# A fused retention and rational feed-forward kernel: in steps 8 to 21, u moves into attention's PSUM banks and the steps get an order of their own

## The chip, the cores and the metric

The kernel runs on one core of one Trainium2 chip. The metric is the device time of one execution in microseconds. Five engines work side by side, each through its own list of instructions in order, and wait for each other by semaphores: TensorE (PE, with its weight loads as PEld) multiplies, VectorE (DVE), ScalarE (ACT) and GpSimd (POOL) work element by element, SyncE (SP) issues the DMAs.

## The reference

Attention without softmax but with a decay, then a feed-forward layer whose activation is a quotient of two polynomials:

```python
scores = scale * np.matmul(q, k.transpose(0, 1, 3, 2))      # 8 x 8 heads, 576 positions of 64
ret = scores * Dmat                                          # gamma ** (i - j) for i >= j, else 0
x = np.matmul(ret, v)                                        # regrouped to 4608 x 512
h = x @ w_in                                                 # 512 -> 2048
P = a[0] + a[1] * h + a[2] * h**2 + a[3] * h**3
Q = 1.0 + np.abs(b[0]) * np.abs(h) + np.abs(b[1]) * h**2
out = (P / (Q + 1e-06)) @ w_out                              # 2048 -> 512
```

## The kernel before

The 4608 rows are 9 blocks of 512 rows. Attention makes x in 36 units of 128 rows, four to a block. The feed-forward layer works block by block (b) and, within a block, through 16 slices of 128 columns of the hidden layer (f). One pair (b, f) is a **step**. The order of the steps is: block 0, f 0 to 7 (steps 0 to 7); block 1, f 0 to 15 (steps 8 to 23); block 0, f 8 to 15 (steps 24 to 31); then blocks 2 to 8. Weights arrive as pairs of float32 words of float64 numbers and have to be put together and split into a high and a low part on the chip; this goes on until step 23, one piece of weight a step.

Operands of the products are kept as high and low parts, so each product is done three times: `gemm1` has 12 matmuls into the PSUM tile h, `gemm2` 12 into acc. PSUM has eight banks: two for h (tile pool `ps_h`, two buffers), four for acc (`ps_acc`), two for attention (`ps_at`, one tile "at" of 2 x 512). No unit of attention is worked on between step 7 and step 22 (list `SCORES`: 5, then 23), so the tile "at" lies unused there.

What one step computes, with the names that the profile shows:

- `ffn_p`: ScalarE writes p<-h (Identity with scale a3 and bias a2) and u<-h (Abs); VectorE p<-p,h (p times h).
- `ffn_p2`: VectorE p<-p,ab_sb,h, after which h's bank is free.
- `ffn_v`: ScalarE v<-u,absb (b1 u + b0), then VectorE v<-v,u (v times u). So v is Q - 1.
- `ffn_r`, for the step before: ScalarE u<-v,lnb (Ln) and u<-u,lnb (Exp): u becomes about 1/Q.
- `ffn_q`, for the step before: VectorE p<-p,ab_sb,u (p becomes P times that), v<-v,u (Q times that), p<-v,p (one Newton step). Below they are q1, q2 and q3.
- `ffn_hi`, `ffn_lo`, for the step before that: ScalarE g<-p rounds p to the high part; the low part g<-p,g is done by GpSimd for the steps up to 23, by VectorE later.
- `gemm2`, three or four steps behind `gemm1` (`lag`).

A piece of weight is prepared by a generator, `split_weight`: `start` is ScalarE's c<-bits; `split0` VectorE's TENSOR_SCALAR c<-c; `split1` VectorE's first c<-bits,c (low word) and `split2` its second (the sign; both have one form); `split3` ScalarE's w<-c and GpSimd's w<-c,w.

The order on each engine is the order in which the code records the instructions: `InOrder` keeps it (line 63, which is why all rows of the profile carry L63). Within a step it is a list of names that `run` goes through: `FIRST` up to step 23, `DENSE` up to step 31, then `REST`, and `END` after the last step. u and v lie in the pool `el` (two buffers in SBUF), p in `el3` (three), g in `gp` (three).

Of the kernel before, what the change touches and what calls it, by code (L numbers as in the profile page):

```python
# [12 lines left out]
F32 = mybir.dt.float32  # L13
# [8 lines left out]
P = 128  # L22
# [7 lines left out]
NF = DFF // P  # L30
# [2 lines left out]
BEFORE = "split1 start scale_q scale_v scores decay outputs split2 add fade keep_hi keep_lo split3 split0".split()  # L33
FIRST = (
    "split1 gemm1 outputs ffn_p split2 ffn_hi keep_hi ffn_lo gemm2 ffn_r scale_q split3 add fade keep_lo start ffn_p2"
    " scale_v scores decay split0 ffn_q ffn_v"
).split()
DENSE = (
    "gemm1 outputs keep_hi split1 add fade keep_lo ffn_p split2 split0 ffn_v scale_q ffn_hi ffn_r ffn_lo scale_v gemm2"
    " ffn_p2 scores decay split3 ffn_q"  # L40
).split()
REST = (
    "gemm1 ffn_p outputs keep_hi add fade keep_lo ffn_hi ffn_p2 ffn_lo scores decay scale_q scale_v ffn_v gemm2 ffn_r ffn_q"
).split()
END = "ffn_r ffn_hi gemm2 ffn_lo ffn_q".split()

STARTS_BEFORE = [0, 1, 1, 2, 2]
STARTS = [1, 1, 2, 1, 2] + [1] * 19
# [1 line left out]
SCORES = [1, 3, 5, 23, 25, 27, 29, *range(2 * NF, (NB - 1) * NF, 4)]  # L50
# [16 lines left out]
def retention_ffn(ctx: ExitStack, tc: tile.TileContext, qkv, w_in, w_out, ab, masks, gq, gv, out):  # L67
# [23 lines left out]
    ps_at = ctx.enter_context(tc.tile_pool(name="ps_at", bufs=1, space=PSUM))  # L91
# [208 lines left out]
    els = {}  # L300
    gs = {}
    accs = {}
    part = []
    spare = {}

# [11 lines left out]
    def ffn_p(b, f):  # L317

        h = hs[b, f]
        u, v, p = els[b, f] = [  # L320
            (el3 if t == "p" else el).tile([P, 512], F32, tag=t, name=f"{t}{b}_{f}") for t in "uvp"
        ]
        act.activation(p, h, AF.Identity, bias=a2, scale=a3)
        act.activation(u, h, AF.Abs)
        dve.tensor_tensor(p, p, h, ALU.mult)
# [2 lines left out]
        p = els[b, f][2]  # L328
        dve.scalar_tensor_tensor(p, p, a1, hs.pop((b, f)), ALU.add, ALU.mult)

    def ffn_v(b, f):

        u, v, p = els[b, f]
        act.activation(v, u, AF.Identity, bias=b0, scale=b1)
        dve.tensor_tensor(v, v, u, ALU.mult)

    def ffn_r(b, f):
# [5 lines left out]
    def ffn_q(b, f):  # L343

        u, v, p = els[b, f]
        dve.scalar_tensor_tensor(p, p, a0, u, ALU.add, ALU.mult)
        dve.scalar_tensor_tensor(v, v, QC, u, ALU.add, ALU.mult)
        dve.scalar_tensor_tensor(p, v, 2.0, p, ALU.subtract, ALU.mult)

    def place(b, f):  # L350
# [54 lines left out]
    half = NF // 2  # L405
    first = half + NF
    runs = [(0, 0, half), (1, 0, NF), (0, half, NF)] + [(b, 0, NF) for b in range(2, NB)]
    steps = [(b, f, f == r0, f == r1 - 1) for b, r0, r1 in runs for f in range(r0, r1)]
    at = {s[:2]: i for i, s in enumerate(steps)}

    def lag(i):

        return 4 if NF // 2 <= i < first - 2 or i >= len(steps) - 8 else 3
# [6 lines left out]
    def load_weights(n):  # L420
        for k in [k for _, k in zip(range(n), loads)]:
            load_weight(k)
# [12 lines left out]
    def run(names, todo):  # L435
        todo |= {f"split{j}": (split_step, j) for j in range(4)}
        for name in names:
            if name in todo:
                todo[name][0](*todo[name][1:])
# [43 lines left out]
    for i in range(len(steps) + lag(len(steps))):  # L483
        this, prev, prev2 = (steps[j][:2] if 0 <= j < len(steps) else None for j in (i, i - 1, i - 2))
        todo = {"gemm2": (products, i), "start": (split_start, STARTS[i] if i < first else 0)}

        out_n = None
        if due and this and i >= due[0][1]:
            out_n = due.pop()[0]
            todo |= {f.__name__: (f, out_n) for f in (keep_hi, add, keep_lo, fade)}  # L490
            todo["outputs"] = (put_out, out_n)
        if i in SCORES:
            todo |= {f.__name__: (f, nxt) for f in (scores, decay)}
            due.append((nxt, i + (1 if i < 2 * NF else 2)))
            nxt += 1
        if i + 1 in SCORES:
            todo |= {f.__name__: (f, nxt) for f in (scale_q, scale_v)}
        if this:
            todo |= {f.__name__: (f, *this) for f in (gemm1, ffn_p, ffn_p2, ffn_v)}
        if prev:  # L500
            todo |= {f.__name__: (f, *prev) for f in (ffn_r, ffn_q)}
        if prev2:
            todo |= {"ffn_hi": (ffn_hi, *prev2), "ffn_lo": (ffn_lo, *prev2, i - 2 < first)}
        run(END if not this else FIRST if i < first else DENSE if i < 2 * NF else REST, todo)
        load_weights(2)


# [48 lines left out]
```

## Time and profile before

| | |
|---|---|
| Median of 3 runs | 981.95 us (980.52 to 983.37) |
| The profiled execution | 983.9 us, its span 982.1 us |
| Mean granted clock of TensorE | 0.980 |
| Busy over the whole span | PE 925.9, DVE 841.0, ACT 712.9, POOL 168.8 us |

A line of the timeline reads: start and length in us, engine, line, operation, output<-inputs by the program's names (without buffer numbers), shape, how many in a row, and in brackets how long the engine sat idle before it and what ended that. A line of groups reads: the same names, count, busy time in us, mean ns of one, idle time before them. A line of stages reads: the stretch, its length, for each engine the busy time and the number of instructions, TensorE's granted clock, the DMA share and GB/s. A line of waits reads: who waited for whom, us in total, how often, the longest.

### The profile page before, as it was taken

What the parts mean: (1) busy time and instruction counts of PE and PEld (TensorE: products, weight loads), DVE (VectorE), ACT (ScalarE), POOL (GpSimd) and SP (SyncE); (2) the same over time, 40 slices, a digit from 0 to 9 for tenths busy, and PEclk for the clock granted to TensorE, in tenths of its full rate; (3) what the DMA queues carried; (4) which work ended last, traced back from release to release, by engine and by line L of the source; (5) the groups of instructions that cost most, each with busy time, mean ns of one, the idle gap of its engine ahead of it and who ended that gap; (6) DMA issues with size and microseconds to landing.
All of it is one profiled execution on the core that took longest, in us unless ns stands there. A gap on an engine that the chain in (4) does not pass through costs nothing.

```text
span 982.1 us, 16128 instructions
## 1 busy us (share of the span) xinstructions
PE 925.9 (94%) x6234; PEld 749.2 (76%) x6234; DVE 841.0 (86%) x1261; ACT 712.9 (73%) x1274; POOL 168.8 (17%) x200
## 2 busy tenths in 40 slices
PE   6669887889999999999999999999999999999997
PEld 6547765667788888888888888888888888888886
DVE  3999988998788988888888888888888888888895
ACT  5477677776766777877787777777777777777775
POOL 4545434344011111101111111101111111100000
PEclk9788999998999999999999999999999999999999
DMA  9945000002212111220121112110211121001001
GB/s 343 407 168 213 3 0 1 1 1 86 86 44 86 44 45 43 87 65 22 44 87 43 44 44 86 44 58 29 87 44 43 44 86 44 2 1 43 0 1 44
DMA packets 20557, 65.44 MB, mean 67 GB/s; under 512 B 2304, under 2 KB 2432, under 8 KB 20480
## 3 DMA queue, kind: packets, MB, share of 16 engines
q1 hardware_dynamic: 20480, 64.41, 18.4%
q8 instruction: 49, 0.80, 0.3%
q14 instruction: 28, 0.23, 0.1%
HBM read 54.96 MB, written 9.44 MB: 66 GB/s over the span
## 4 chain that ended last, share of the span: by engine, by line
PE 77%; DVE 12%; ACT 4%; issue 3%; DMA 2%; POOL 1%; SPq 0%; POOLq 0%; ACTq 0%
PE acc L63 35%; PE h L63 33%; PE ps L63 9%; DVE c L63 6%; DVE p L63 4%; DVE v L63 1%; ACT c L63 1%; DMA kv<-in_qkv 1%; ACT kv L63 1%; POOL w L63 1%; DMA mask_sb<-in_masks 1%; ACT u L63 0%; ACT w L63 0%; ACT o L63 0%; DVE s L63 0%
## 5 line engine op out<-in xcount | busy, mean ns | idle before, releaser
L63 PE MATMUL acc<-w,g 128*128 128x512 f32 x1632 | 404.5, 397 | 5.2 <-ACT o L63 4.0
L63 PE MATMUL h<-xhi,w 128*128 128x512 f32 x1152 | 381.5, 392 | 18.1 <-DVE p L63 16.0
L63 PEld LDWEIGHTS acc<-w,g 128*128 128x128 f32 x1632 | 304.7, 190 | 75.9 <-ACT o L63 4.9
L63 PEld LDWEIGHTS h<-xhi,w 128*128 128x128 f32 x1152 | 217.2, 189 | 69.1 <-DVE p L63 21.0
L63 PE MATMUL h<-xlo,w 128*128 128x512 f32 x576 | 225.4, 391 | 0.2 <-DVE xlo L63 0.2
L63 ACT ACTIVATE p<-h,ab_sb 128x512 f32<-128x512 f32 x144 | 111.4, 773 | 105.9 <-PE h L63 105.8
L63 ACT ACTIVATE u<-h 128x512 f32<-128x512 f32 x144 | 85.9, 596 | 76.6 <-DVE v L63 75.0
L63 DVE SCALAR_TENSOR_TENSOR p<-p,ab_sb,u 128x512 f32<-128x512 f32 x144 | 107.8, 749 | 25.4 <-ACT u L63 22.1
L63 PEld LDWEIGHTS h<-xlo,w 128*128 128x128 f32 x576 | 108.7, 189 | 22.5 <-DVE xlo L63 0.5
L63 DVE TENSOR_TENSOR v<-v,u 128x512 f32<-128x512 f32 x144 | 99.7, 692 | 27.9 <-ACT v L63 27.7
L63 DVE TENSOR_TENSOR p<-p,h 128x512 f32<-128x512 f32 x144 | 98.9, 687 | 27.9 <-ACT u L63 27.4
L63 ACT ACTIVATE v<-u,absb 128x512 f32<-128x512 f32 x144 | 116.0, 805 | 0.3
L63 DVE SCALAR_TENSOR_TENSOR p<-p,ab_sb,h 128x512 f32<-128x512 f32 x144 | 107.1, 744 | 3.1
L63 ACT ACTIVATE u<-u,lnb 128x512 f32<-128x512 f32 x144 | 104.3, 724 | 4.7
L63 DVE SCALAR_TENSOR_TENSOR p<-v,p 128x512 f32<-128x512 f32 x144 | 99.6, 692 | 5.0
L63 ACT ACTIVATE u<-v,lnb 128x512 f32<-128x512 f32 x144 | 102.8, 714 | 0.2 <-DVE v L63 0.2
L63 DVE SCALAR_TENSOR_TENSOR v<-v,u 128x512 f32<-128x512 f32 x144 | 99.2, 689 | 0.0
L63 DVE TENSOR_TENSOR g<-p,g 128x512 fp32r<-128x512 f32 x112 | 91.6, 818 | 1.4 <-ACT g L63 1.4
L63 ACT ACTIVATE g<-p 128x512 fp32r<-128x512 f32 x136 | 85.7, 630 | 8.7 <-DVE p L63 3.3
L63 POOL TENSOR_TENSOR S_sb<-S_sb,gv_sb 128x256 f32<-128x256 f32 x32 | 20.4, 638 | 403.4 <-DVE S_sb L63 402.5
L63 ACT ACTIVATE kv<-kv,gv_sb 128x64 f32<-128x64 f32 x288 | 72.6, 339 | 11.5 <-DMA gv_sb<-in_gv 6.1
L63 DVE TENSOR_TENSOR s<-ps,mask_sb 64x256 f32<-64x256 f32 (+1 forms) x108 | 55.0, 509 | 11.6 <-DMA mask_sb<-in_masks 7.9
(36 smaller groups left out, 649.3 us busy)
## 6 DMA issues: line engine op xcount, KB each, us to landing
qk<-in_qkv SPq DMA_DIRECT2D x36, 512.0 KB, 4.9
kv<-in_qkv SPq DMA_DIRECT2D x36, 512.0 KB, 4.1
bits<-in_w_in SPq DMA_DIRECT2D x16, 512.0 KB, 10.2
bits<-in_w_out SPq DMA_DIRECT2D x16, 512.0 KB, 10.2
out<-o SPq DMA_DIRECT2D x16, 512.0 KB, 3.5
out<-o SPq DMA_DIRECT2D x4, 256.0 KB, 2.4
gq_sb<-in_gq SPq DMA_DIRECT2D x1, 256.0 KB, 2.8
mask_sb<-in_masks SPq DMA_DIRECT2D x1, 160.0 KB, 6.2
```

The lines of the kernel that those rows point to most:

```text
L63: return lambda *a, **k: self.tc.keep_in_program_order(method(*a, **k))
```

## The change

Three things, all for steps 8 to 21:

1. At step 8 the code takes a tile "at" from `ps_at` (name `free_at`) and uses its two banks in turn for u, which otherwise lies in SBUF. At step 22 (`SCORES[3] - 1`) it stops; u of step 22 lies in SBUF again, and attention takes the banks in step 23.
2. `ffn_v` is cut into `ffn_va` (ScalarE's v<-u) and `ffn_v` (VectorE's v times u), and `ffn_q` into `ffn_q` (q1, q2) and `ffn_q3`. In the old lists the parts stand side by side as before.
3. Steps 8 to 21 follow a new list, `MID`, in place of `FIRST`.

```diff
 FIRST = (
     "split1 gemm1 outputs ffn_p split2 ffn_hi keep_hi ffn_lo gemm2 ffn_r scale_q split3 add fade keep_lo start ffn_p2"
-    " scale_v scores decay split0 ffn_q ffn_v"
+    " scale_v scores decay split0 ffn_q ffn_q3 ffn_va ffn_v"
+).split()
+MID = (
+    "split1 split2 gemm1 ffn_p ffn_r ffn_hi ffn_lo split3 ffn_va gemm2 ffn_p2 ffn_q ffn_v ffn_q3 start split0"
 ).split()
...
         u, v, p = els[b, f] = [
+            free_at[f % 2] if t == "u" and free_at else
             (el3 if t == "p" else el).tile([P, 512], F32, tag=t, name=f"{t}{b}_{f}") for t in "uvp"
         ]
...
-    def ffn_v(b, f):
+    def ffn_va(b, f):
 
         u, v, p = els[b, f]
         act.activation(v, u, AF.Identity, bias=b0, scale=b1)
+
+    def ffn_v(b, f):
+        u, v, p = els[b, f]
         dve.tensor_tensor(v, v, u, ALU.mult)
...
         dve.scalar_tensor_tensor(v, v, QC, u, ALU.add, ALU.mult)
+
+    def ffn_q3(b, f):
+        u, v, p = els[b, f]
         dve.scalar_tensor_tensor(p, v, 2.0, p, ALU.subtract, ALU.mult)
...
+        if i == half:
+            ps = ps_at.tile([P, 2, 512], F32, tag="at", name="free_at")
+            free_at.extend((ps[:, 0], ps[:, 1]))
+        elif i == SCORES[3] - 1:
+            free_at.clear()
-        run(END if not this else FIRST if i < first else DENSE if i < 2 * NF else REST, todo)
+        run(END if not this else MID if free_at else FIRST if i < first else DENSE if i < 2 * NF else REST, todo)
```

What VectorE's list holds for step 11 (block 1, f 3) before the change; names end in block and slice, then a running number, so p1_3 is p of step 11 and p1_2 that of step 10:

```order
L63 SCALAR_TENSOR_TENSOR c0_10_1236<-bits0_10_955,c0_10_1236 128x512
L63 TENSOR_TENSOR p1_3_1265<-p1_3_1265,h1_3_1250 128x512
L63 SCALAR_TENSOR_TENSOR c0_10_1236<-bits0_10_955,c0_10_1236 128x512
L63 SCALAR_TENSOR_TENSOR p1_3_1265<-p1_3_1265,ab_sb_95,h1_3_1250 128x512
L63 TENSOR_SCALAR c0_11_1294<-c0_11_1294 128x512
L63 SCALAR_TENSOR_TENSOR p1_2_1211<-p1_2_1211,ab_sb_95,u1_2_1209 128x512
L63 SCALAR_TENSOR_TENSOR v1_2_1210<-v1_2_1210,u1_2_1209 128x512
L63 SCALAR_TENSOR_TENSOR p1_2_1211<-v1_2_1210,p1_2_1211 128x512
L63 TENSOR_TENSOR v1_3_1264<-v1_3_1264,u1_3_1263 128x512
```

And in the changed kernel, the same step:

```order
L66 SCALAR_TENSOR_TENSOR c0_10_1240<-bits0_10_955,c0_10_1240 128x512 x2
L66 TENSOR_TENSOR p1_3_1263<-p1_3_1263,h1_3_1249 128x512
L66 SCALAR_TENSOR_TENSOR p1_3_1263<-p1_3_1263,ab_sb_95,h1_3_1249 128x512
L66 SCALAR_TENSOR_TENSOR p1_2_1210<-p1_2_1210,ab_sb_95,free_at_1099 128x512
L66 SCALAR_TENSOR_TENSOR v1_2_1209<-v1_2_1209,free_at_1099 128x512
L66 TENSOR_TENSOR v1_3_1262<-v1_3_1262,free_at_1099 128x512
L66 SCALAR_TENSOR_TENSOR p1_2_1210<-v1_2_1209,p1_2_1210 128x512
L66 TENSOR_SCALAR c0_11_1297<-c0_11_1297 128x512
```

The two c<-bits now stand together at the head (one row, x2); the five operations that read h or free_at (PSUM) follow each other; q3 and the TENSOR_SCALAR, which read SBUF alone, stand behind them and so just ahead of the next step's two c<-bits.

ScalarE's list for the same step 11 before (o are the two copies of block 0's first sums, in this step only):

```order
L63 ACTIVATE p1_3_1265<-h1_3_1250,ab_sb_95 128x512
L63 ACTIVATE u1_3_1263<-h1_3_1250 128x512
L63 ACTIVATE g1_1_1270<-p1_1_1157 128x512
L63 ACTIVATE o0_0_7_1285<-acc0_0_0_721 128x1024
L63 ACTIVATE o0_1_7_1287<-acc0_0_1_722 128x1024
L63 ACTIVATE u1_2_1209<-v1_2_1210,lnb_108 128x512
L63 ACTIVATE u1_2_1209<-u1_2_1209,lnb_108 128x512
L63 ACTIVATE w0_10_1291<-c0_10_1236 128x512
L63 ACTIVATE c0_11_1294<-bits0_11_957 128x512
L63 ACTIVATE v1_3_1264<-u1_3_1263,absb_96 128x512
```

And in the changed kernel:

```order
L66 ACTIVATE p1_3_1263<-h1_3_1249,ab_sb_95 128x512
L66 ACTIVATE free_at_1099<-h1_3_1249 128x512
L66 ACTIVATE free_at_1099<-v1_2_1209,lnb_108 128x512
L66 ACTIVATE free_at_1099<-free_at_1099,lnb_108 128x512
L66 ACTIVATE g1_1_1269<-p1_1_1157 128x512
L66 ACTIVATE w0_10_1272<-c0_10_1240 128x512
L66 ACTIVATE v1_3_1262<-free_at_1099,absb_96 128x512
L66 ACTIVATE o0_0_7_1288<-acc0_0_0_721 128x1024
L66 ACTIVATE o0_1_7_1290<-acc0_0_1_722 128x1024
L66 ACTIVATE c0_11_1297<-bits0_11_957 128x512
```

Ln and Exp moved ahead of g, v ahead of o and of the next c<-bits, and o behind v. TensorE's, GpSimd's and SyncE's lists keep their order.

More of the change, by code (lines that the diff above doesn't have):

```diff
@@ L35 @@
     "split1 gemm1 outputs ffn_p split2 ffn_hi keep_hi ffn_lo gemm2 ffn_r scale_q split3 add fade keep_lo start ffn_p2"
-    " scale_v scores decay split0 ffn_q ffn_v"
+    " scale_v scores decay split0 ffn_q ffn_q3 ffn_va ffn_v"
+).split()
+MID = (
+    "split1 split2 gemm1 ffn_p ffn_r ffn_hi ffn_lo split3 ffn_va gemm2 ffn_p2 ffn_q ffn_v ffn_q3 start split0"
 ).split()
 DENSE = (
-    "gemm1 outputs keep_hi split1 add fade keep_lo ffn_p split2 split0 ffn_v scale_q ffn_hi ffn_r ffn_lo scale_v gemm2"
-    " ffn_p2 scores decay split3 ffn_q"
+    "gemm1 outputs keep_hi split1 add fade keep_lo ffn_p split2 split0 ffn_va ffn_v scale_q ffn_hi ffn_r ffn_lo scale_v gemm2"
+    " ffn_p2 scores decay split3 ffn_q ffn_q3"
 ).split()
 REST = (
-    "gemm1 ffn_p outputs keep_hi add fade keep_lo ffn_hi ffn_p2 ffn_lo scores decay scale_q scale_v ffn_v gemm2 ffn_r ffn_q"
+    "gemm1 ffn_p outputs keep_hi add fade keep_lo ffn_hi ffn_p2 ffn_lo scores decay scale_q scale_v ffn_va ffn_v gemm2 ffn_r ffn_q ffn_q3"
 ).split()
-END = "ffn_r ffn_hi gemm2 ffn_lo ffn_q".split()
+END = "ffn_r ffn_hi gemm2 ffn_lo ffn_q ffn_q3".split()
 STARTS_BEFORE = [0, 1, 1, 2, 2]
@@ L302, in retention_ffn @@
     accs = {}
+    free_at = []
     part = []
@@ L329, in ffn_p2 @@
         dve.scalar_tensor_tensor(p, p, a1, hs.pop((b, f)), ALU.add, ALU.mult)
+    def ffn_va(b, f):
+        u, v, p = els[b, f]
+        act.activation(v, u, AF.Identity, bias=b0, scale=b1)
     def ffn_v(b, f):
         u, v, p = els[b, f]
-        act.activation(v, u, AF.Identity, bias=b0, scale=b1)
         dve.tensor_tensor(v, v, u, ALU.mult)
@@ L498, in retention_ffn @@
         if this:
-            todo |= {f.__name__: (f, *this) for f in (gemm1, ffn_p, ffn_p2, ffn_v)}
+            todo |= {f.__name__: (f, *this) for f in (gemm1, ffn_p, ffn_p2, ffn_va, ffn_v)}
         if prev:
-            todo |= {f.__name__: (f, *prev) for f in (ffn_r, ffn_q)}
+            todo |= {f.__name__: (f, *prev) for f in (ffn_r, ffn_q, ffn_q3)}
         if prev2:
             todo |= {"ffn_hi": (ffn_hi, *prev2), "ffn_lo": (ffn_lo, *prev2, i - 2 < first)}
-        run(END if not this else FIRST if i < first else DENSE if i < 2 * NF else REST, todo)
+        if i == half:
[4 more added lines that the diff above has]
+        run(END if not this else MID if free_at else FIRST if i < first else DENSE if i < 2 * NF else REST, todo)
         load_weights(2)
```

## The prediction

> **What bounds the kernel now.** First the busy time by stage (engines in the order PE, PEld, DVE, ACT, POOL, then PE's granted clock, DMA share, GB/s), since the change touches only steps 8 to 21:
>
> ```profile
> 109.00:211.00 102.00, 83.71 (x345) 64.31 (x343) 92.45 (x128) 74.75 (x115) 40.00 (x28) 0.98 0.00 1
> 211.00:250.00 39.00, 31.95 (x228) 24.68 (x229) 32.77 (x49) 29.35 (x64) 16.59 (x17) 0.91 0.19 62
> 250.00:982.00 732.00, 727.04 (x4830) 591.71 (x4828) 626.96 (x953) 539.14 (x946) 61.16 (x98) 1.00 0.14 48
> ```
>
> Steps 8 to 21 lie between 109 and 211 us. There VectorE is busy 92.45 of 102 us and TensorE 83.71; nothing is being loaded. From 250 us on TensorE is busy 727 of 732 us. So time won in the first stretch reaches the end whole if the stretch behind it (211 to 250) keeps its length: the long last stage only starts earlier. Next, who waits for whom from 109 to 211:
>
> ```profile
> PE h L63 <- DVE p L63: 16.0, 11, 1.5
> ACT u L63 <- DVE v L63: 15.2, 14, 1.1
> ACT w L63 <- DVE c L63: 10.7, 13, 0.8
> DVE c L63 <- ACT c L63: 9.1, 14, 1.4
> ```
>
> TensorE waits for VectorE (p, which frees h's bank), ScalarE waits for it twice, and VectorE waits for ScalarE's c once a step, 0.59 us. One step of VectorE, ScalarE and GpSimd in the timeline (start, length):
>
> ```profile
> 149.66 1.07 DVE L63 TENSOR_SCALAR c<-c 128x512 int32<-128x512 int32 x1 [0.59 <-ACT c L63]
> 150.65 0.74 DVE L63 SCALAR_TENSOR_TENSOR p<-p,ab_sb,u 128x512 f32<-128x512 f32 x1
> 151.31 0.68 DVE L63 SCALAR_TENSOR_TENSOR v<-v,u 128x512 f32<-128x512 f32 x1
> 152.03 0.69 DVE L63 SCALAR_TENSOR_TENSOR p<-v,p 128x512 f32<-128x512 f32 x1
> 152.64 0.68 DVE L63 TENSOR_TENSOR v<-v,u 128x512 f32<-128x512 f32 x1
> 153.24 0.68 DVE L63 SCALAR_TENSOR_TENSOR c<-bits,c 128x512 int32<-128x512 int32 x1
> 153.84 0.68 DVE L63 TENSOR_TENSOR p<-p,h 128x512 f32<-128x512 f32 x1
> 154.44 1.18 DVE L63 SCALAR_TENSOR_TENSOR c<-bits,c 128x512 int32<-128x512 int32 x1
> 155.54 0.73 DVE L63 SCALAR_TENSOR_TENSOR p<-p,ab_sb,h 128x512 f32<-128x512 f32 x1
> 156.87 1.07 DVE L63 TENSOR_SCALAR c<-c 128x512 int32<-128x512 int32 x1 [0.59 <-ACT c L63]
> ```
>
> ```profile
> 148.45 0.63 ACT L63 ACTIVATE w<-c 128x512 fp32r<-128x512 f32 x1 [0.82 <-DVE c L63]
> 148.98 0.64 ACT L63 ACTIVATE c<-bits 128x512 f32<-128x512 f32 x1
> 149.53 0.80 ACT L63 ACTIVATE v<-u,absb 128x512 f32<-128x512 f32 x1
> 150.24 0.76 ACT L63 ACTIVATE p<-h,ab_sb 128x512 f32<-128x512 f32 x1
> 152.09 0.60 ACT L63 ACTIVATE u<-h 128x512 f32<-128x512 f32 x1 [1.08 <-DVE v L63]
> 152.75 0.63 ACT L63 ACTIVATE g<-p 128x512 fp32r<-128x512 f32 x1
> 153.36 0.72 ACT L63 ACTIVATE u<-v,lnb 128x512 f32<-128x512 f32 x1
> 154.11 0.72 ACT L63 ACTIVATE u<-u,lnb 128x512 f32<-128x512 f32 x1
> ```
>
> ```profile
> 149.16 1.29 POOL L63 TENSOR_TENSOR w<-c,w 128x512 fp32r<-128x512 f32 x1 [1.29 <-ACT w L63]
> 153.52 1.55 POOL L63 TENSOR_TENSOR g<-p,g 128x512 fp32r<-128x512 f32 x1 [3.07 <-issue]
> 156.36 1.30 POOL L63 TENSOR_TENSOR w<-c,w 128x512 fp32r<-128x512 f32 x1 [1.29 <-ACT w L63]
> ```
>
> A step takes 156.87 - 149.66 = 7.21 us. Its circle: the second c<-bits (I call it c sign, the first c low) ends at 155.62, then w and c on ScalarE, then the TENSOR_SCALAR, then all of VectorE's row up to the next c sign. Two of its members are long for one reason. c sign (1.18) has c low's form (0.68); it starts at 154.44, while GpSimd's g runs until 155.07, and ends 0.55 after that. The TENSOR_SCALAR starts at 149.66, GpSimd's w ends at 150.45, and it ends 0.28 after that; with GpSimd idle the same operation took
>
> ```profile
> 18.56 0.42 DVE L63 TENSOR_SCALAR c<-c 128x512 int32<-128x512 int32 x1
> ```
>
> So a VectorE operation that reads SBUF alone stands still until GpSimd's has ended: 1.18 - 0.68 = 0.50 and 1.07 - 0.42 = 0.65 us a step. p<-p,h, with h in PSUM, runs from 153.84 to 154.52 inside the same g and takes its usual 0.68: an operand in PSUM sets it free of GpSimd.
>
> **The change, part by part.** *Number of operations:* the same on every engine; no DMA is added, and the lists of TensorE, GpSimd and SyncE keep their order. *u in PSUM:* three more operations of VectorE (q1 = p<-p,u; q2 = v<-v,u; and v*u) get a PSUM operand, and four of ScalarE's write or read one. What that does to ScalarE's length is read from two copies of one size, out of SBUF and out of PSUM:
>
> ```profile
> L63 ACT ACTIVATE g<-p 128x512 fp32r<-128x512 f32 x136 | 85.7, 630 | 8.7 <-DVE p L63 3.3
> ```
>
> ```profile
> L63 ACT ACTIVATE xhi<-ps 128x512 fp32r<-128x512 f32 x36 | 21.5, 596 | 35.5 <-PE ps L63 29.2 <-DVE S_sb L63 6.2
> ```
>
> VectorE: 0.68 for p<-p,h in the timeline above, 0.68 for v*u, nothing. ScalarE: the copy out of PSUM takes 596 ns against 630, so I take 0.03 off the two operations that now read u from PSUM (Exp and v<-u); ScalarE writing to PSUM is in no row, and I take 0 for it, between -0.03 and +0.03 an operation. *A rule against this:* the Trainium skill (Perfetto Trace Analysis, Optimizing Scalar/DVE Operations) gives VectorE about 60 ns of access on SBUF and 125 on PSUM, and ScalarE 93 and 51. By it, an estimate, three operations would cost VectorE 0.2 us more a step, 2.5 us in 13; the trace's 0.68 against 0.68 bears out no such price for VectorE, while ScalarE's 596 against 630 agrees in direction.
>
> *The new order on VectorE* is c low, c sign, p*h, p2, q1, q2, v*u, q3, TENSOR_SCALAR. From start to start an operation takes 0.60 (150.65 to 151.31: 0.66 with a pointer scalar), and 0.72 where the next reads its result (151.31 to 152.03). Without GpSimd: 0.72 + 0.60 + 0.72 + 0.66 + 0.66 + 0.60 + 0.60 + 0.61 + 0.45 = 5.62 us, VectorE's floor per step.
>
> *A new wait.* The framework tracks the PSUM tile as a whole, both banks: in the built program ScalarE's u of step i+1 waits for VectorE's v*u of step i, and VectorE's q1 of step i-1 waits for ScalarE's v<-u of step i, though they touch different banks. Queued behind the former are Ln, Exp, g, w, v; behind the latter q2 and v*u, for which ScalarE waits. That closes a circle. Let V be the end of v*u. ScalarE: handover 0.04, u 0.63 (0.60 and the gap of 0.03 ahead of a dependent operation, as between Ln and Exp), Ln 0.75, Exp 0.60, g 0.53, w 0.53, v 0.77 = 3.85. VectorE: handover 0.04, q1 0.66, q2 0.60, v*u 0.68 = 1.98. Together **5.83 us**, more than the floor of 5.62, so this circle sets the step. What must fit beside it: c sign ends at V + 2.38 (q3 at V - 0.08, TENSOR_SCALAR V + 0.53, c low V + 0.98, c sign V + 1.70), and w on ScalarE would start at V + 2.55: 0.17 us to spare. GpSimd's g starts when ScalarE's g ends, V + 2.65, and with w behind it is done by V + 5.2; the next q3 comes at V + 5.75. So both GpSimd operations fall on VectorE's five PSUM operations, and the 0.50 and 0.65 us go. ScalarE's c and p stand between v and the next u with 0.8 us to spare.
>
> *What is late next.* Here are the stretch's two ends, and TensorE around step 11, where the sums of block 0's first half are copied out (o):
>
> ```profile
> 108.56 0.69 DVE L63 TENSOR_TENSOR v<-v,u 128x512 f32<-128x512 f32 x1
> ...
> 210.37 0.69 DVE L63 TENSOR_TENSOR v<-v,u 128x512 f32<-128x512 f32 x1
> ```
>
> ```profile
> 131.91 4.27 PE L63 MATMUL acc<-w,g 128*128 128x512 f32 x12 [2.21 <-ACT o L63]
> ...
> 139.10 2.88 PE L63 MATMUL acc<-w,g 128*128 128x512 f32 x12
> ```
>
> ```profile
> L63 ACT ACTIVATE o<-acc 128x1024 f32<-128x1024 f32 x2 | 1.9, 1014 | 0.0
> ```
>
> Twelve matmuls take 2.88 - 0.39 for eleven distances, 0.226 each, so 24 need 5.43 us: TensorE stays under 5.83. In step 11 the two o now stand behind v on ScalarE, not behind g. They take 1.9 us, of which 0.8 to 0.9 was spare: 1.0 us late (no DMA hangs on them, the sums stay in SBUF). With V that of step 10, TensorE has done all ahead of the next block's first product at V + 0.8 and waits until the first o is done at V + 4.7: some 4 us idle against 2.21. After the 2.21 the same 12 matmuls took 4.27 instead of 2.88; I expect 1.4 to 3.4 us lost on TensorE, against 0.6 us of slack of the h that ScalarE wants: 0 to 2.6, I take 0.7. Together 1.7.
>
> *Sum.* Before: from v*u of step 7 (ends 109.25) to v*u of step 21 (ends 211.06) 101.8 us. After: step 8 is mixed, since q1 and q2 of step 7 still read u in SBUF and meet GpSimd's g and w, 0.5 longer, 6.3; 13 x 5.83 = 75.8; o 1.7; together 83.8. Behind it q3 and TENSOR_SCALAR come ahead of step 22's c low, which starts at V + 0.98 instead of V - 0.08: 1.1 lost. 101.8 - 83.8 - 1.1 = **16.9 us**. In step 23 the scores need the banks back, after q2 of step 21. In step 22's old order that is 6.0 us in (3.63 from c low to TENSOR_SCALAR, 2.33 on to q2's end); TensorE's product ahead of the scores needs GpSimd's g of step 22 and 2.7 us of its own, and is not done sooner, so I take 0; without that cover it is 1 to 2 us. The profiled execution took 983.9 us with a span of 982.1; the runs' median is 981.95, and I take the gain off that: **965.0 us**.
>
> **The rivals.**
> 1. *Part is given back* between 211 and 250 us, where TensorE idles 7 of 39 us at a clock of 0.91: its lead over VectorE changes there, the banks come back late, or another half-clock stretch (1.4 to 3.4 us, as above) is added. Price 4 to 9 us: 969 to 974. For it: that stretch is a chain of waits; against it: nearly all hang on VectorE, which shifts as a whole.
> 2. *The collision stays in part.* If GpSimd's w slips by 0.6 us it meets q3, and then TENSOR_SCALAR and c sign as today. With 0.64 + 0.65 us of waits c sign ends at V + 3.67, w starts there, and the step takes 6.94: 13 x 1.11 = 14.4 less gain, 979.5. Against it: 0.5 us of room on that side.
> 3. *Slower.* The same place goes wrong wholly: c sign lies on the new circle (w waits for it, then v, q1, q2, v*u), so each us that q3, TENSOR_SCALAR, c low and c sign stand still behind GpSimd, less 0.17, lengthens every step. Both operations of GpSimd in that stretch are 2.6 us: a step of 8.2, 13 x 2.4 = 31 us, 996. It decides from a step of 7.13 on, so from 1.5 us of waits; today's are 1.15. For it: GpSimd's g starts only 0.27 us behind c sign's end. Against it: if g came earlier, it would meet one operation, not four.
> 4. *The change does not do what it says:* PSUM operands do not set q1, q2 and v*u free, because v or p in SBUF hold the port all the same. Then little is won beyond the order: near 982. Against it stands p<-p,h, which is of that very kind.
>
> **How the numbers follow.** Forecast 0.66 (steps of 5.62 to 6.2: 962 to 970, with o's 0 to 2.6 from 960 to 971); rival 1 0.12; rival 2 0.10; rival 3 0.06; rival 4 0.06. A measurement here can tell about 0.3% (2.9 us) from no change. Faster: 0.66 + 0.12 + 0.06 of rival 2 = 0.84; same: 0.04 of rival 2 + 0.05 of rival 4 = 0.09; slower: 0.06 + 0.01 = 0.07. The range 958 to 975 takes in the forecast and rival 1 and leaves out the others, about 0.2.
>
> **What would show it.** Right: between 109 and 195 us TENSOR_SCALAR c takes 0.42 and both c<-bits 0.68; VectorE's period is 5.8, its short idle time lies before q1, ended by ScalarE's v; ScalarE's lies before u, ended by VectorE's v; GpSimd's g takes 1.3 and lies under p2, q1, q2; TensorE waits once some 4 us for o. Wrong: a c<-bits or q3 over 1 us, w on ScalarE waiting for c, a period over 6.3, or a stretch behind it longer than today's 39 us.

## The result

The changed kernel takes **964.8 us** (964.0 to 965.6, four runs) against 981.4 (980.5 to 983.4) for the kernel before: a ratio of 0.982 [0.980, 0.983]. A second set of five runs gave 965.9 against 982.9, 0.982 [0.980, 0.984]. The forecast was 965.0, the range 958 to 975. The profiled execution of the changed kernel took 965.2 us, its span is 963.4.

First the busy time by stage in the changed kernel (columns as before: PE, PEld, DVE, ACT, POOL, then PE's clock, DMA share, GB/s), cut where steps 8 to 21 and the stretch behind them now lie:

```profile
110.00:193.00 83.00, 76.69 (x328) 62.06 (x327) 80.10 (x127) 70.80 (x115) 36.13 (x28) 0.98 0.00 1
193.00:231.00 38.00, 34.01 (x244) 26.62 (x243) 34.52 (x49) 29.22 (x63) 16.65 (x17) 0.96 0.17 60
231.00:963.00 732.00, 727.38 (x4831) 591.91 (x4829) 626.65 (x953) 539.74 (x947) 61.01 (x98) 1.00 0.14 48
```

Steps 8 to 21 fill 83 us in place of 102. The stretch behind is 38 us (39 before), the last stage 732 as before, so what was won reaches the end. VectorE is now busy 80.1 of 83 us, TensorE 76.7. The waits in the first of these stretches (engine, tile, what it waited for; total us, times, longest):

```profile
ACT free_at L66 <- DVE v L66: 8.8, 11, 1.8
...
PE acc L66 <- ACT o L66: 3.6, 1, 3.6
PE h L66 <- DVE p L66: 2.7, 2, 1.6
...
DVE p L66 <- ACT v L66: 1.0, 1, 1.0
```

Of the four rows that stood here before, ScalarE's w and VectorE's c (9 to 11 us each, and with them the 0.59 us a step) are gone, and TensorE's wait for p fell from 16.0 to 2.7 us. ScalarE's u (free_at) still waits for VectorE in nearly every step, 8.8 us in place of 15.2, now as a member of the circle that the prediction named. The last row is one time alone, behind the two o copies of step 11. One step of VectorE, from the start of one v*u to the next, then ScalarE's row and GpSimd's beside it:

```profile
151.23 0.68 DVE L66 TENSOR_TENSOR v<-v,free_at 128x512 f32<-128x512 f32 x1
151.83 0.68 DVE L66 SCALAR_TENSOR_TENSOR p<-v,p 128x512 f32<-128x512 f32 x1
152.43 0.42 DVE L66 TENSOR_SCALAR c<-c 128x512 int32<-128x512 int32 x1
152.89 1.42 DVE L66 SCALAR_TENSOR_TENSOR c<-bits,c 128x512 int32<-128x512 int32 x2
154.22 0.68 DVE L66 TENSOR_TENSOR p<-p,h 128x512 f32<-128x512 f32 x1
154.94 0.75 DVE L66 SCALAR_TENSOR_TENSOR p<-p,ab_sb,h 128x512 f32<-128x512 f32 x1
155.72 0.75 DVE L66 SCALAR_TENSOR_TENSOR p<-p,ab_sb,free_at 128x512 f32<-128x512 f32 x1
156.38 0.68 DVE L66 SCALAR_TENSOR_TENSOR v<-v,free_at 128x512 f32<-128x512 f32 x1
156.98 0.68 DVE L66 TENSOR_TENSOR v<-v,free_at 128x512 f32<-128x512 f32 x1
```

```profile
151.95 0.58 ACT L66 ACTIVATE free_at<-h 128x512 f32<-128x512 f32 x1 [0.52 <-DVE v L66]
152.56 0.69 ACT L66 ACTIVATE free_at<-v,lnb 128x512 f32<-128x512 f32 x1
153.29 0.66 ACT L66 ACTIVATE free_at<-free_at,lnb 128x512 f32<-128x512 f32 x1
153.87 0.62 ACT L66 ACTIVATE g<-p 128x512 fp32r<-128x512 f32 x1
154.39 0.62 ACT L66 ACTIVATE w<-c 128x512 fp32r<-128x512 f32 x1
154.92 0.77 ACT L66 ACTIVATE v<-free_at,absb 128x512 f32<-128x512 f32 x1
```

```profile
154.63 1.31 POOL L66 TENSOR_TENSOR g<-p,g 128x512 fp32r<-128x512 f32 x1 [3.20 <-issue]
155.87 1.32 POOL L66 TENSOR_TENSOR w<-c,w 128x512 fp32r<-128x512 f32 x1
```

The step takes 156.98 - 151.23 = 5.75 us. The two c<-bits (one row, x2) take 1.42 together and the TENSOR_SCALAR 0.42: nothing there stands still any more. GpSimd works from 154.63 to 157.19, and all that VectorE does meanwhile (p2, q1, q2, most of v*u) reads PSUM and takes its usual 0.68 to 0.75. The circle can be followed from row to row: v*u ends at 151.91, u starts at 151.95, Ln, Exp, g, w, v follow without a gap to 155.69, q1 starts at 155.72, and the next v*u ends at 157.66, 5.75 later.

### The profile page after: what moved, and what is told of

Its sections match the earlier page's. It is cut to its first block, busy times and chain, and to the rows that moved or that the text cites. A ratio compares the mean times of both kernels' runs of the same rounds, so it can differ in the third digit from the quotient of the medians.

```text
span 963.4 us, 16126 instructions
## 1 busy us (share of the span) xinstructions
PE 922.9 (96%) x6234; PEld 750.2 (78%) x6234; DVE 830.7 (86%) x1261; ACT 708.9 (74%) x1274; POOL 164.4 (17%) x200
## 4 chain that ended last, share of the span: by engine, by line
PE 79%; DVE 8%; ACT 6%; DMA 5%; issue 1%; POOL 1%; SPq 0%; ACTq 0%; POOLq 0%
PE acc L66 36%; PE h L66 34%; PE ps L66 8%; DMA bits<-in_w_in 3%; DVE p L66 3%; DVE c L66 2%; ACT free_at L66 2%; DVE v L66 2%; DMA bits<-in_w_out 1%; ACT v L66 1%; ACT w L66 1%; DMA qk<-in_qkv 1%; ACT g L66 1%; ACT o L66 0%; DVE s L66 0%
## 5 line engine op out<-in xcount | busy, mean ns | idle before, releaser
L66 ACT ACTIVATE u<-h 128x512 f32<-128x512 f32 x130 | 77.5, 596 | 59.9 <-DVE v L66 58.3
L66 DVE SCALAR_TENSOR_TENSOR p<-p,ab_sb,u 128x512 f32<-128x512 f32 x130 | 97.8, 753 | 25.7 <-ACT u L66 22.5
L66 DVE TENSOR_TENSOR v<-v,u 128x512 f32<-128x512 f32 x130 | 91.1, 701 | 28.5 <-ACT v L66 28.4
L66 ACT ACTIVATE v<-u,absb 128x512 f32<-128x512 f32 x130 | 104.7, 806 | 1.2 <-DVE p L66 0.9
L66 ACT ACTIVATE u<-u,lnb 128x512 f32<-128x512 f32 x130 | 94.2, 724 | 4.2
L66 ACT ACTIVATE u<-v,lnb 128x512 f32<-128x512 f32 x130 | 92.8, 714 | 2.0 <-DVE v L66 2.0
L66 DVE SCALAR_TENSOR_TENSOR v<-v,u 128x512 f32<-128x512 f32 x130 | 90.7, 698 | 0.0
```

Of the source, the lines that this page charges most:

```text
L66: return lambda *a, **k: self.tc.keep_in_program_order(method(*a, **k))
```

## The experiments

Two things changed at once: where u lies, and the order. **T1** says: VectorE operations that read only SBUF stand still behind GpSimd; the order puts GpSimd under five operations, and PSUM operands make these five immune; both are needed. **R1** says that the order alone does it, by taking ScalarE's w and c out of VectorE's path. Each half was run alone, and each order with GpSimd made quiet.

### The order alone

```diff
-            free_at[f % 2] if t == "u" and free_at else
...
-            ps = ps_at.tile([P, 2, 512], F32, tag="at", name="free_at")
-            free_at.extend((ps[:, 0], ps[:, 1]))
+            free_at.extend((None, None))
```

> Steps 8 to 21 in the new order (v ahead of the quotient, g and w behind Exp), with u left in SBUF in its two buffers. Theory T1 (the gain is the collisions with GpSimd that go, and they go because the operations that run beside GpSimd have an operand in PSUM): g and w (2.6 us back to back) now lie on q1, q2 and v*u, which read SBUF alone; as in step 8 of the changed kernel (q1 1.31, q2 1.78 in place of 0.75 and 0.68) some 1.6 us of standing still a step, so a step of about 7.2 to 7.4 and a time within 6 us of the kernel before, 977 to 986. Rival R1 (the order does it, by taking ScalarE's w and c out of VectorE's path; where u lies matters little): a step of 5.6 to 5.8, c sign and TENSOR_SCALAR at 0.68 and 0.42, q1 and q2 at 0.75 and 0.68, 962 to 966.

Measured: 975.3 us, ratio 0.991 [0.988, 0.994], between the two. VectorE from p<-p,h to q1, with the q1 of the next step, and the GpSimd operations beside it:

```profile
158.71 0.68 DVE L66 TENSOR_TENSOR p<-p,h 128x512 f32<-128x512 f32 x1
159.43 0.75 DVE L66 SCALAR_TENSOR_TENSOR p<-p,ab_sb,h 128x512 f32<-128x512 f32 x1
160.09 1.66 DVE L66 SCALAR_TENSOR_TENSOR p<-p,ab_sb,u 128x512 f32<-128x512 f32 x1
...
166.65 1.67 DVE L66 SCALAR_TENSOR_TENSOR p<-p,ab_sb,u 128x512 f32<-128x512 f32 x1
```

```profile
158.57 1.38 POOL L66 TENSOR_TENSOR g<-p,g 128x512 fp32r<-128x512 f32 x1 [3.93 <-issue]
159.91 1.29 POOL L66 TENSOR_TENSOR w<-c,w 128x512 fp32r<-128x512 f32 x1
```

A step is 166.65 - 160.09 = 6.56 us. The collision is there, as T1 says, but in one operation: q1 starts at 160.09 inside w (159.91 to 161.20) and ends 0.55 after it, 1.66 in place of 0.75. T1's 1.6 us a step was too much: it took step 8 as the pattern, where g and w both fall on q1 and q2. In the settled steps g (158.57 to 159.95) comes earlier and lies on p*h and p2, which read h in PSUM and take their usual 0.68 and 0.75. So half of GpSimd's work is covered by operands that were in PSUM before the change. R1 falls too: q1 loses 0.91 us a step.

### The order alone, GpSimd quiet; the old order, GpSimd quiet

```diff
-        pool.tensor_tensor(w[:, 1, :], cf, w[:, 0, :].bitcast(F32), ALU.subtract)
+        if quiet:
+            pool.memset(w[:, 1, :].bitcast(F32), 0.0)
+        else:
+            pool.tensor_tensor(w[:, 1, :], cf, w[:, 0, :].bitcast(F32), ALU.subtract)
...
+        if quiet:
+            pool.memset(g[:, 1, :].bitcast(F32), 0.0)
-        if by_pool:
+        elif by_pool:
```

quiet is set in steps 8 to 21, once in the kernel before and once in the order alone.

> The kernel before, but in steps 8 to 21 GpSimd's two subtractions a step (the low parts of w and g) are replaced by fills with zero, which read nothing: the low parts are left out of the products there. T1, if a fill does not hold VectorE up: c sign back to 0.68, TENSOR_SCALAR to 0.42, 1.15 us a step less with the order and SBUF as they were: a step of 6.0 to 6.1 and 965 to 968 (13 or 14 steps by 1.15 = 15 to 16 us); so the collisions are most of the change's gain and the order's own share is about 0.3 a step. Rival R1 (the collisions cost nothing on the path, the 0.59 us wait for ScalarE's c does): a step of 6.9 or more, 977 to 982.

> The new order with u in SBUF as in order_alone, and GpSimd's two subtractions replaced by fills with zero as in before_quiet (the low parts are left out there). T1: nothing collides and u lies in two separately tracked buffers, so VectorE's row back to back sets the step, 5.6 to 5.7, and the time is 962 to 965; together with order_alone this shows the PSUM operands to be nothing but a cure of the collision. R1: the same as order_alone. If ScalarE's faster work on PSUM were part of the gain, the step would be 5.8 or more.

Measured: 967.8 us, 0.983 [0.981, 0.985], for the old order and 959.4, 0.975 [0.974, 0.977], for the new one, the former inside T1's range, the latter 2.6 us below it. Two things account for that: step 8 has nothing to collide with either and took 4.58 us (6.26 in the order alone), and the o copies cost nothing on the path there, the two steps behind them took 5.66 and 5.64. VectorE's rows of the old order, a step apart, with c sign between them:

```profile
145.32 0.43 DVE L63 TENSOR_SCALAR c<-c 128x512 int32<-128x512 int32 x1 [0.60 <-ACT c L63]
...
149.46 0.69 DVE L63 SCALAR_TENSOR_TENSOR c<-bits,c 128x512 int32<-128x512 int32 x1
...
151.40 0.43 DVE L63 TENSOR_SCALAR c<-c 128x512 int32<-128x512 int32 x1 [0.60 <-ACT c L63]
```

The TENSOR_SCALAR takes 0.43 in place of 1.07, c sign 0.69 in place of 1.18, and the wait of 0.60 for ScalarE's c is still there; the step is 6.08. GpSimd's fills of 0.52 us lie beside p2 in this order. A fill beside an operation that reads only SBUF can be seen further on in the changed kernel, where g<-p,g has moved to VectorE:

```profile
263.69 0.67 POOL L66 MEMSET s<- 64x256 f32 x2 [5.26 <-PE acc L66]
```

```profile
263.79 0.68 DVE L66 TENSOR_TENSOR g<-p,g 128x512 fp32r<-128x512 f32 x1
```

The operation starts behind the first fill, takes 0.68 us and ends at 264.47, 0.11 after the fills' end (264.36); beside a subtraction the end came 0.55 after GpSimd's. So a fill holds VectorE up by nothing that can be seen here. The Trainium skill (SBUF — State Buffer, Who interferes with whom) has this rule: a VectorE instruction with two SBUF inputs contends with a GpSimd instruction that reads SBUF and not with one that only writes it, and with at most one SBUF input it does not contend, except in the modes that take a second port, for which the page names tensor_scalar among others. The traces agree: c sign 1.18 beside a subtraction and 0.69 without one, g<-p,g 0.68 beside a fill, q1 1.66 with u in SBUF and 0.75 with u in PSUM, and the TENSOR_SCALAR, with one SBUF input, 1.07 beside a subtraction and 0.43 without (that it ran in such a mode stands in no trace). And the new order:

```profile
150.00 0.42 DVE L66 TENSOR_SCALAR c<-c 128x512 int32<-128x512 int32 x1
...
155.63 0.42 DVE L66 TENSOR_SCALAR c<-c 128x512 int32<-128x512 int32 x1
```

Here the step is 5.63, VectorE's row back to back, with u in SBUF: without a collision PSUM is not needed. The four cases make a table of steps (us):

| | old order | new order |
|---|---|---|
| u in SBUF, GpSimd as it is | 7.21 | 6.56 |
| u in SBUF, GpSimd quiet | 6.08 | 5.63 |
| collision | 1.13 | 0.93 |

So of the 1.46 us by which a step became shorter, 0.45 is the order's own (6.08 to 5.63; the wait of 0.60 for c goes, and two operations in place of one now stand directly behind one whose result they read, at 0.72 in place of 0.60). The collisions were worth 1.13; the order alone saves 0.20 of it, the PSUM operands the other 0.93, and 0.12 is given back to the circle (5.63 to 5.75). 0.45 + 1.13 - 0.12 = 1.46. The kernel before with a quiet GpSimd is nearly as fast as the changed one (0.983 and 0.982 of before).

### PSUM alone, as one tile and as two

```diff
-        run(END if not this else MID if free_at else FIRST if i < first ...
+        run(END if not this else FIRST if i < first ...
```

> u in the PSUM tile in steps 8 to 21, in the order of before. T1: c sign and the TENSOR_SCALAR have no operand in PSUM and meet GpSimd's g and w as they did (1.18 and 1.07), VectorE still waits 0.59 for ScalarE's w and c, so a step of 7.1 to 7.3 and 979 to 984. Rival R2 (u in PSUM does it, wherever GpSimd's work lies, by making ScalarE's reads and writes shorter and VectorE free): a step under 6.5 and a time under 973.

Measured: 996.7 us, 1.013 [1.012, 1.015]: slower than before, which no theory said. VectorE's TENSOR_SCALAR in two steps and q2 between them, then ScalarE's v:

```profile
145.89 1.07 DVE L66 TENSOR_SCALAR c<-c 128x512 int32<-128x512 int32 x1 [0.59 <-ACT c L66]
...
147.54 0.67 DVE L66 SCALAR_TENSOR_TENSOR v<-v,free_at 128x512 f32<-128x512 f32 x1
...
154.12 1.07 DVE L66 TENSOR_SCALAR c<-c 128x512 int32<-128x512 int32 x1 [0.59 <-ACT c L66]
```

```profile
148.25 0.78 ACT L66 ACTIVATE v<-free_at,absb 128x512 f32<-128x512 f32 x1 [2.39 <-DVE v L66]
```

The step is 8.23. ScalarE's v<-u of a step starts at 148.25, 0.04 after VectorE's q2 of the step before ends (148.21), having waited 2.39 us, although it reads the other bank. T2: the tile framework, not the chip, orders them, because both banks are one tile. Then two tiles must take it away:

```diff
-            ps = ps_at.tile([P, 2, 512], F32, tag="at", name="free_at")
-            free_at.extend((ps[:, 0], ps[:, 1]))
+            at_stack.close()
+            ps_u = at_stack.enter_context(tc.tile_pool(name="ps_u", bufs=1, space=PSUM))
+            free_at.extend(ps_u.tile([P, 512], F32, tag=f"u{j}", name=f"free{j}") for j in range(2))
...
+        elif i == SCORES[3]:
+            at_stack.close()
+            ps_at = at_stack.enter_context(tc.tile_pool(name="ps_at2", bufs=1, space=PSUM))
```

> psum_alone (the order of before, u in PSUM) with the two banks as two tiles. psum_alone's step was 8.23 us, 1.0 more than before, and ScalarE's v<-u started only when VectorE's q2 of the step before had ended. T2 (that wait comes from the tracking of both banks as one tile, and is why v had to go ahead of the quotient): it goes, and the step is before's 7.2 less at most 0.1 for ScalarE's shorter Exp and v, 980 to 984. Rival (PSUM operands themselves slow the old order, by a contention of ScalarE and VectorE on PSUM): the step stays at 7.8 or more, 990 or more.

Measured: 981.4 us, 0.999 [0.998, 1.000].

```profile
148.42 1.06 DVE L66 TENSOR_SCALAR c<-c 128x512 int32<-128x512 int32 x1 [0.60 <-ACT c L66]
...
155.60 1.07 DVE L66 TENSOR_SCALAR c<-c 128x512 int32<-128x512 int32 x1 [0.59 <-ACT c L66]
```

The step is 7.18 and the TENSOR_SCALAR takes 1.06 as before the change. So T2 holds: the whole tile's tracking cost 1.0 us a step in the old order, and PSUM operands by themselves are worth nothing there, since GpSimd's work lies beside c sign and the TENSOR_SCALAR there. In the changed kernel v stands ahead of the quotient in the program, so that q1 waits for v and not v for q2 of the step before; that edit was not run by itself.

### The change with two tiles

> The change, but the two banks that hold u are two tiles of their own, so that u of one step no longer waits for v*u of the step before, nor q1 for the v<-u beside it. T1: the circle of 5.75 us that these waits close is gone and VectorE's row back to back sets the step, 5.62 to 5.65 as in order_quiet; 13 steps by 0.11 = 1.4 us, a time of 962 to 964 against 964.8 for the change. Rival: the step of 5.75 is set by something else (ScalarE's own row, or VectorE's reads of PSUM being longer than of SBUF); then it stays 5.75 and the time 964 to 966.

Measured: 963.4 us, 0.980 [0.979, 0.982]. Two v*u one step apart:

```profile
155.71 0.68 DVE L66 TENSOR_TENSOR v<-v,free 128x512 f32<-128x512 f32 x1
...
161.33 0.68 DVE L66 TENSOR_TENSOR v<-v,free 128x512 f32<-128x512 f32 x1
```

5.62, VectorE's floor as the prediction worked it out, and the wait of ScalarE's u is gone: the circle was the tracking's, and it cost 0.13 us a step. From v*u of step 7 to that of step 21 the profiled execution took 80.4 us in place of 82.0.

### One step earlier; both; GpSimd quiet in the changed kernel

```diff
-        if i == half:
+        if i == half - 1:
```

> The change, begun one step earlier, in step 7 (one tile for both banks, as in the change). T1: step 8 took 6.24 us because q1 and q2 of step 7 still read u from SBUF and stand still behind GpSimd (1.31 and 1.78 in place of 0.75 and 0.68); step 7 itself took 7.2 us in the old order. With both in the new form steps 7 and 8 take 5.75 to 6.3 each: 1.0 to 2.0 us less than the change, 962.5 to 964. Rival: the head, up to there paced by other work (attention's outputs in step 6), gives the time back in step 7; 964.5 to 966.

> two_tiles and from7 together. T1: the two gains add, 2.4 to 3.4 us less than the change, 961 to 963. Rival: they share a limit (TensorE's matmuls of 5.43 us a step, or the o copies in step 11, which come earlier in relation to ScalarE's work), 963 to 965.

> The changed kernel with GpSimd's two subtractions a step replaced by fills with zero in steps 8 to 21 (the low parts of w and g are left out there). T1 (in the changed order GpSimd's work lies wholly under operations with a PSUM operand and costs nothing): the step stays 5.75, set by the circle; only step 8 loses its collision (q1 and q2 of step 7), some 1.6 us, 962.5 to 964.5 against 964.8. Rival (PSUM operands free VectorE only in part, or GpSimd's traffic also slows ScalarE): the step falls below 5.70 and the time below 962.

Measured: 963.9 us, 0.981 [0.979, 0.982], from step 7 on; 962.9, 0.979 [0.977, 0.981], with two tiles as well; 961.5, 0.979 [0.977, 0.981], with GpSimd quiet. The first two lie inside T1's ranges. From v*u of step 6 to that of step 21 the profiled executions took 89.2 us (the change), 87.6 (two tiles), 88.0 (from step 7) and 87.0 (both): 1.6 and 1.2 saved, and together 2.2, not 2.8. This is no limit that the two share: the version of the next section, which is the same up to step 21, took 86.0 us there, 3.2 less than the change. The steps behind the o copies differ: 6.9 and 6.4 us in the one trace, 6.1 and 6.1 in the other, in place of 5.6. TensorE waited 3.47 us for o in both, and its 12 matmuls after the wait took 5.49 in the one and 4.61 in the other (2.88 in other steps), a matter of its clock (last section). For step 8, q1 and q2 of step 7 in the changed kernel, and then with GpSimd quiet:

```profile
112.77 1.31 DVE L66 SCALAR_TENSOR_TENSOR p<-p,ab_sb,u 128x512 f32<-128x512 f32 x1
114.01 1.77 DVE L66 SCALAR_TENSOR_TENSOR v<-v,u 128x512 f32<-128x512 f32 x1
```

```profile
111.92 0.75 DVE L66 SCALAR_TENSOR_TENSOR p<-p,ab_sb,u 128x512 f32<-128x512 f32 x1
112.58 0.69 DVE L66 SCALAR_TENSOR_TENSOR v<-v,u 128x512 f32<-128x512 f32 x1
```

The two stand still for 0.56 and 1.09 us, 1.65 together; with GpSimd quiet step 8, from v*u to v*u, took 4.57 in place of 6.25 (q3 and the TENSOR_SCALAR lie ahead of it in step 7's old order, so it is shorter than the floor). The later steps, but for the two behind the o copies, stayed at 5.75, as T1 has it: in the changed order GpSimd costs nothing from step 9 on. The time fell 1 us below T1's range and below the rival's 962, but the step doesn't bear out the rival. The two profiled executions lie 4.0 us apart: 1.4 in this stretch, 1.8 behind it, and 0.9 ahead of it, where both kernels hold the same instructions. Of the 1.8, 1.6 come in one place, where TensorE waited 1.81 and 1.75 us for a later o and the 12 matmuls after it took 4.61 and 3.02. A second profiled execution of the changed kernel, GpSimd as it is, has 3.02 there too (last section), so it was not the quiet GpSimd that won this.

### A version that beats it

With two tiles, begun in step 7, step 22 was put in the new order as well:

```diff
+MID_SCORES = (
+    "split1 split2 gemm1 ffn_p ffn_r ffn_hi ffn_lo split3 ffn_va gemm2 ffn_p2 ffn_q ffn_v ffn_q3 scale_q start scale_v split0"
+).split()
...
-        run(END if not this else MID if free_at else FIRST if i < first ...
+        run(END if not this else MID if free_at else MID_SCORES if i == SCORES[3] - 1 else FIRST if i < first ...
```

> The changed kernel itself, beside the next one on the same chip: 964 to 966.

> both, and step 22 in the new order too, with the two scalings for attention's next scores behind the rest. From the end of v*u of step 21 to that of step 22 both took 8.64 us: c sign 1.2 and TENSOR_SCALAR 1.44 meet GpSimd, and VectorE waits 0.6 for ScalarE's c. In the new order these go, but ScalarE's row with the scaling (2.0) is 7.3 us long and u of step 22 lies in SBUF. T1: 1 to 1.5 us less than both, 960.5 to 962.5. Rival: the scaling, now behind c, makes p of step 23 late by as much, and nothing is left of it; 962 to 964.5.

Measured on one chip: 965.9 us for the change, 960.8 for this version, 0.978 [0.976, 0.980] of the kernel before. In the changed kernel step 22 still has the old order and its collisions. In this version u of step 22 lies in SBUF, and its v*u stands still behind GpSimd:

```profile
187.67 0.68 DVE L69 TENSOR_TENSOR v<-v,free 128x512 f32<-128x512 f32 x1
...
193.29 1.67 DVE L69 TENSOR_TENSOR v<-v,u 128x512 f32<-128x512 f32 x1
```

From the end of v*u of step 21 to that of step 22 it is 194.96 - 188.35 = 6.61, where two tiles from step 7 took 8.64: 2.0 us less. In step 23 the later scaling gives 1.2 of it back, as the rival said, but not all. The intervals of this version (0.976 to 0.980) and of two tiles from step 7 (0.977 to 0.981) overlap; against the change (0.980 to 0.984 in the same set) it is faster by about 0.5%.

## Why the prediction was right

*The cause* held at each step. The collisions were 0.50 + 0.65 = 1.15 us a step by the prediction's reading of the trace, and 1.13 by the quiet run. Operands in PSUM free q1, q2 and v*u (0.75, 0.68, 0.68 beside GpSimd). The new order puts both GpSimd operations under the five, and the tracking of the whole tile closes a circle that sets the step. Rival 4 (PSUM operands don't free VectorE) falls by those rows; rivals 2 and 3 (the collision stays, in part or wholly on the circle) by the 0.42 of the TENSOR_SCALAR and the 1.42 of two c<-bits in steps 9 to 21. The place was close: w started 0.08 us after c sign's end (154.39 and 154.31), where 0.17 was forecast.

*The sizes.* Four terms, forecast and measured in the profiled execution:

| term | forecast | measured | in a second execution (965.9 us) |
|---|---|---|---|
| step 8 | 6.3 | 6.25 | 6.25 |
| 13 steps | 13 x 5.83 = 75.8 | 13 x 5.75 = 74.7 | 74.7 |
| o in step 11 | 1.7 | 1.0 | 2.6 |
| c low of step 22, after v*u of step 21 ends | 0.98 | 0.97 | 0.97 |

Step 8 came out right by two errors that cancel. The forecast took a step of 5.83 and 0.5 for the collision; q1 and q2 stood still for 1.65 us, three times as much, and with GpSimd quiet the step took 4.57.

The circle was mis-sized by 0.08 us: writing to PSUM was counted at 0. These are ScalarE's four operations on u in the changed kernel (line, engine, operation; busy us, mean ns; idle time and its cause):

```profile
L66 ACT ACTIVATE v<-free_at,absb 128x512 f32<-128x512 f32 x14 | 10.8, 769 | 0.0
...
L66 ACT ACTIVATE free_at<-v,lnb 128x512 f32<-128x512 f32 x13 | 9.0, 693 | 0.4
...
L66 ACT ACTIVATE free_at<-free_at,lnb 128x512 f32<-128x512 f32 x13 | 8.6, 662 | 0.4
L66 ACT ACTIVATE free_at<-h 128x512 f32<-128x512 f32 x13 | 7.6, 586 | 8.8 <-DVE v L66 8.8
```

Before they took 803, 725, 724 and 600 ns on average in steps 8 to 21: v, which reads PSUM, lost 34, as forecast (30); Ln, which only writes there, lost 32, and Exp, which does both, 62. So for Ln a write is worth as much as v's read, at the end of the bound of 0.03 that the prediction gave. It is not so for every operation: u (Abs), which read PSUM before too and now writes it, lost only 14. VectorE's price for PSUM was nothing, as taken: v*u 685 ns before, 679 after; the rule of the Trainium skill (Perfetto Trace Analysis, Optimizing Scalar/DVE Operations), 125 ns of access on PSUM against 60 on SBUF, is not borne out for VectorE here.

o cost 1.0 us in the first execution: TensorE waited 3.6 us (some 4 forecast) and VectorE's q1 1.0 for v, by the waits above. In the second execution it cost 2.6, after the same wait of 3.62: the 12 matmuls behind it took 5.49 in place of 4.34, ScalarE's p<-h then waited 2.40 us for h in place of 0.85, and the step after that took 7.39 in place of 5.83. So what was taken as 0.7, TensorE's loss, was close to 0 once and 1.6 once; the idea of a loss with a range was right, and the value in it a guess. The range itself doesn't follow from the numbers beside it (1.4 to 3.4 less 0.6 of slack makes 0.8 to 2.8, not 0 to 2.6), and no run shows the 3.4: measured were 1.5 and 2.6 us more than the 2.88 of other steps.

*The sum.* The stretch from v*u of step 7 to c low of step 22 was 101.7 us in the profiled execution of before; it became 18.75 us shorter in the first execution of the changed kernel and 17.2 in the second, where 16.9 was forecast. The circle gave 1.1 more than forecast both times; o gave 0.7 more and 0.9 less. The medians differ by 16.6 and 17.0. That 965.0 came within 0.2 us of the median is luck in part: single runs of the same kernel spread from 963 to 967 us, and of the one before from 980 to 985. For the changed kernel the two traces show where such a spread comes from: 1.6 us at the o of step 11, and 1.6 us the other way at a later o. The profiled execution of before, 2 us above its median, has the longer time at the later o as well (4.60 us for the 12 matmuls); that its faster runs have the shorter one is likely and not shown, as there is one trace of it.

What lies behind c low of step 22 took 771.1 us before, and 770.3 and 768.5 in the changed kernel, so nothing was given back: rival 1 falls, and with its price of 4 to 9 us a long way. The banks came back in time, as the prediction took it, but only just: q2 of step 21 ends at 199.46, TensorE's product at 199.51, and the first scores of step 23 start at 199.56.

## What to carry to other kernels

When VectorE is the bound and a GpSimd operation overlaps it, compare each VectorE row with the same operation elsewhere: a row that ends a fixed time after GpSimd's end stood still for it. Then look for VectorE operations with a PSUM operand and order the work so that GpSimd's lies beside those, or let it write and not read. Give each PSUM bank that is used by itself its own tile: as parts of one tile, two banks are ordered against each other, for reads too, and that cost from 0.13 to 1.0 us a step here.

## What had not been expected

The same wait of TensorE is not always followed by the same clock. These are the two profiled executions of the changed kernel, of 965.2 and 965.9 us, in this order in each pair. In a pair the instructions are the same and the waits nearly so, first behind the o of step 11, then behind the later o:

```profile
132.60 4.34 PE L66 MATMUL acc<-w,g 128*128 128x512 f32 x12 [3.62 <-ACT o L66]
```

```profile
133.52 5.49 PE L66 MATMUL acc<-w,g 128*128 128x512 f32 x12 [3.62 <-ACT o L66]
```

```profile
230.32 4.61 PE L66 MATMUL acc<-w,g 128*128 128x512 f32 x12 [1.81 <-ACT o L66]
```

```profile
232.62 3.02 PE L66 MATMUL acc<-w,g 128*128 128x512 f32 x12 [1.79 <-ACT o L66]
```

Over these matmuls the granted clock was 0.67 and 0.50 in the first pair, 0.63 and 1.00 in the second. Neither execution had the shorter time in both places. The Trainium skill (TensorE: Matmul & The Clock Gate, What's actually happening) describes a window of about 3.4 us that runs freely and halves the clock after an idle one; that the phase decides fits these rows, and the 0.50 fits the half, though here 1.8 us of waiting were enough, and no run here measures the window. For a prediction it means that an idle time of 1.8 to 3.6 us has two prices, 1.2 and 1.6 us apart here, which the trace of one execution cannot choose between.

A half of the change can be worse than none: u in PSUM without the order made the kernel 1.3% slower, by a wait between two reads of different banks that no hardware asked for.
